# GpSimd for the low halves of probabilities, ScalarE for centring and scaling, TensorE for seven weight splits: one change to a fused attention, Fourier and MLP kernel

## The chip, the cores and the metric

The kernel runs on one core of a Trainium2 chip. Its time is the device time of the program in microseconds; the time before is the median of 3 runs, 1094.59 us (1094.49 to 1094.82). One more execution was taken by the profiler, and all rows below are from it.

A core has five engines, each with a queue of its own that it works off in order: TensorE (PE for its products, PEld for loading the stationary operand), VectorE (DVE), ScalarE (ACT), GpSimd (POOL) and SyncE (SP), which here issues nearly all DMAs. They wait for each other through semaphores.

## What is computed

```python
# attention, 4 batches x 8 heads, 576 tokens, head size 64
scores = scale * q @ k.T
cum = cumsum(maximum(s, 0));  bias = minimum(-(cum[i] - cum[j]), 0)
scores = where(causal, -1e9, scores + bias)
attn = exp(scores - max);  attn = attn / (sum(attn) + 1e-9)
x = attn @ v                       # heads side by side: 4 x 576 x 512
# first block
u = x + real(fft(fft(x, axis=1), axis=2))
un = (u - mean(u)) / sqrt(var(u) + 1e-6)
u2 = u + maximum(un @ w_ch1, 0) @ w_ch2          # 512 -> 2048 -> 512
# second block
xn = (u2 - mean(u2)) / sqrt(var(u2) + 1e-6) * g_ln
out = u2 + maximum(xn @ w2_ch1, 0) @ w2_ch2
```

The weights arrive as 64 bit floats, the rest as 32 bit floats.

## The kernel before

*Two halves for every number.* Most products run in fp16. A number is held as a high half (its fp16 cast) and a low half (what the cast lost, again fp16), and a product is three products: high by high, high by low, low by high. So there are many pairs of instructions of one shape: ScalarE makes the high half, and VectorE or GpSimd subtracts it from the 32 bit value to make the low half.

*Weights.* The class `Weights` handles the first MLP's weights in 32 pieces of 128x512 (16 of `w_ch1`, 16 of `w_ch2`). `prep` loads each piece as 64 bit words into one of nine staging places, turns it into 32 bit floats with three integer instructions on VectorE (L159, L162, L165), squares it on ScalarE for a common power of two as scale (L176), and calls `split` (L203 on ScalarE for the high half with the scale, L204 on VectorE for the low half, scaled and subtracted in one instruction). `prep` is a generator; its steps are put between the steps of the first batch's attention. The second MLP's weights go through the subclass `Weights7`, whose sums of blocks (seven products in place of eight) GpSimd makes (L304).

*Attention.* A batch is four pairs of heads; a pair is 10 units, one for each of five tiles of queries (A0, A1, M, B1, B0, numbered 0 to 4, with 129, 257, 320, 448 and 576 keys) and each of two heads. For a unit, `emit_bias` writes the masked sums into a score tile on GpSimd (L739, for the batches 1 to 3), three units ahead; `emit_qk` multiplies (fp32 in the batches 0 and 1, L1018; split fp16 in 2 and 3, L756 and L757) and VectorE adds the bias and takes the minimum (L1023, L758); `emit_exp` runs the exponential twice on ScalarE, into the fp16 high half (L781) and in place in fp32 with its sum (L782). One unit later `emit_lo` subtracts the two (L794): on GpSimd for the tiles that `KN["LO_POOL"]` names for the batch, on VectorE for the others. A transposing DMA on SP's queue turns the halves (L798, L806), and five or seven units later `emit_pv` multiplies with v (L826) into one PSUM bank, from which VectorE takes the result (L839). In the batches 2 and 3 the sums must carry the scale of q and k: `scale_cum` multiplies the loaded sums in place (L655), and GpSimd's L739 reads them. Where a tile has fewer keys than its blocks, GpSimd clears the rest of the tile (L775) once the tile's last transpose is through.

*Fourier step and LayerNorm.* `fft_steps` does a batch's transform as products with constant matrices. `emit_ln` normalizes a chunk of up to two tiles of 128 tokens: VectorE takes mean and variance (L338, L339) and an estimate of the inverse root (`p`); VectorE makes the centred and scaled 32 bit tile `un` (L351), ScalarE the same in fp16 from the input (L355), VectorE the low half (L358), and a transposing DMA turns both.

*Streams.* `MlpStream` multiplies a chunk with `w_ch1` (L387), applies the relu and splits (L393 on ScalarE, L394 on VectorE), and multiplies with `w_ch2` (L411). Beside the MLP of batch b run the attention and Fourier steps of the next batches, put between the MLP's steps at a fixed rate. After the last batch's MLP has begun, the second MLP's weights are prepared beside it; then nine chunks run through the second MLP (L453, L481).

*Order.* The program's order is only a priority. A planner that weighs every instruction by its own costs, and knows of the priorities and of the `issue_after` and `urgent` blocks, writes down the queue of each engine at build time. An instruction that is moved to another engine so also changes the order of its neighbours.

Of the kernel before, what the change touches and what calls it, by code (L numbers as in the profile page):

```python
# [26 lines left out]
EXT = [129, 257, 320, 448, 576]  # L27
NKB = [2, 3, 3, 4, 5]
MASKED = -(2.0 ** 120)
KN = {'PVS': (0, 3, 0, 0), 'ORD': ((0, 0, 0), (0, 0, 0), (1, 0, 0), (1, 0, 0)), 'WR4': (1.2, 1.2, 1.2, 1.2), 'W0': 4, 'WRATE': 1.0, 'W2PRE': 18, 'NCONST': 40, 'HOLDN': 1, 'S1': 4, 'S2': 1, 'S1B': 0, 'COST': (1.0, 1.0, 1.0, 1.0, 1.0), 'POOL1': (), 'POOLB': (0, 1, 2, 3, 4, 5, 6, 7), 'QF': (3, 3, 3, 3, 3, 3, 3, 3, 3, 3, 3), 'QL': (1, 1, 1, 1), 'WCALLS': 2, 'WN': 65, 'SPGATE': 0, 'LATE4': 1, 'MARK': 30, 'CJ': (2, 6), 'PVLAG': 7, 'LOLAG': 1, 'PVLAG32': 5, 'PJ32': 4, 'A0OFF': 0, 'A1OFF': 0, 'F0OFF': 300, 'AOFF': (200, 0, 300, 300), 'FOFF': (300, 600, 300, 150), 'LNOFF': (300, 600, 150, 600), 'LOFF': 300, 'PJ': 1, 'PN': 1, 'PL': 6, 'KPREP': 0, 'KPRE': (6, 0, 0), 'KSTEP': ((0, 0, 1), (0, 1), (1,)), 'RATES': (1.9, 1.4, 2.1, 1.2), 'POOLX': (0, 1, 1, 1), 'LO_POOL': ((0, 4, 1, 3, 2), (0, 1, 2, 3), (4,), (0, 1, 2)), 'TAILW': 2, 'LNM': 0, 'LAZY': 8, 'CALLS3': 65, 'N32': 2}  # L30


@with_exitstack
def fused_kernel(ctx: ExitStack, tc, q, k, v, s, wa1, wa2, g_ln, wb1, wb2, tok_c, feat_c, ident_c, rev_c, bias_c, out):
    nc = tc.nc
# [75 lines left out]
    class Weights:  # L111
# [3 lines left out]

        PLACE = [i % 9 for i in range(16)] + [6, 5, 4, 3, 7, 8, 6, 5, 7, 8, 6, 7, 8, 7, 8, 7]

        LIMITS, LAST, HOLD = (11, 15), 16, True

        def __init__(self, pool, pre, w1, w2, g, spare, extra, junk):  # L120
            self.staged = {}
# [56 lines left out]
        def scale(self, w):  # L178
            tot = small.tile([128, 1], F32, tag="wtot", name="wtot")
            nc.vector.tensor_reduce(out=tot, in_=self.fro[:, 16 * w:16 * w + 16], op=ALU.add, axis=AX)  # L180
            all_ = total(tot)
            pow2_scale(self.sc[:, 2 * w:2 * w + 1], self.sc[:, 2 * w + 1:2 * w + 2], all_, self.LIMITS[w])
            if w == 0:
                if self.g is None:
                    self.s1 = [self.sc[:, 0:1]] * KB
                else:
                    nc.vector.tensor_scalar(
                        out=self.gs, in0=self.g, scalar1=self.sc[:, 0:1], scalar2=None, op0=ALU.mult
                    )
# [78 lines left out]
    class Weights7(Weights):  # L268

        LIMITS, LAST, HOLD, PLACE = (10, 14), 8, False, [i % 7 for i in range(32)]

        def __init__(self, pool, pre, w1, w2, g, junk):
            self.staged = {}
# [51 lines left out]
    def emit_ln(ch):  # L327

        n = ch.n
        xs = [ch.get(j) for j in range(n)]
        ch.x = xs
        mv = small.tile([128, 2, 2], F32, tag="mv", name="mv")[:, 0:n, :]
        for j in range(n):
            st = small.tile([128, 6], F32, tag="st", name="st")
            nc.vector.bn_stats(out=st, in_=xs[j])  # L338
            nc.vector.bn_aggr(out=mv[:, j, :], in_=st)  # L339
        va4 = small.tile([128, 8], F32, tag="va", name="va")  # L340
        va, p, d, mp = (va4[:, 2 * i:2 * i + n] for i in range(4))
        nc.vector.tensor_scalar(out=va, in0=mv[:, :, 1], scalar1=1e-6, scalar2=None, op0=ALU.add)
        nc.vector.tensor_scalar(
            out=p.bitcast(I32), in0=va.bitcast(I32), scalar1=-0.5, scalar2=float(0x5F3759DF), op0=ALU.mult, op1=ALU.add
        )
        ch.last = nc.vector.scalar_tensor_tensor(out=mp, in0=mv[:, :, 0], scalar=-1.0, in1=p, op0=ALU.mult, op1=ALU.mult)
        yield
        ch.unT = mpool.tile([128, 8, 256], F16, tag="unT", name="unT")
        for j in range(n):
            un = un_tile[0]()[:, 0:512]  # L350
            nc.vector.tensor_scalar(  # L351
                out=un, in0=xs[j], scalar1=mv[:, j, 0:1], scalar2=p[:, j:j + 1], op0=ALU.subtract, op1=ALU.mult
            )
            u16 = mpool.tile([128, 1024], F16, tag="u16", name="u16")
            nc.scalar.activation(  # L355
                out=u16[:, 0:512], in_=xs[j], func=AF.Identity, scale=p[:, j:j + 1], bias=mp[:, j:j + 1]
            )
            ch.last = nc.vector.tensor_tensor(out=u16[:, 512:1024], in0=un, in1=u16[:, 0:512], op=ALU.subtract)  # L358
            ch.tr = nc.sync.dma_start_transpose(out=ch.unT[:, :, j * 128:(j + 1) * 128], in_=u16)
            yield  # L360

        nc.vector.tensor_tensor(out=d, in0=p, in1=p, op=ALU.mult)
# [224 lines left out]
    def prep_cum():  # L587
# [887 lines left out]
```

## Time and profile before

| | |
|---|---|
| median of 3 runs | 1094.59 us |
| profiled execution | 1095.33 us, its span 1093.6 us |
| TensorE (PE) busy | 967.2 us (88%), 8644 products |
| VectorE (DVE) busy | 720.1 us (66%), 1848 instructions |
| ScalarE (ACT) busy | 580.1 us (53%), 1350 instructions |
| GpSimd (POOL) busy | 415.3 us (38%), 717 instructions |
| mean granted clock of TensorE | 0.95 of full speed |

A share of busy time is a mean over stages with different limits, so the span is cut by what runs in it: up to 165 us the first batch's attention and Fourier step and the first MLP's weights; up to 262 us the second batch's attention beside the first MLP; up to 410 and 550 us the third and the fourth batch's; up to 697 us the rest of the first MLP and the second one's weights; up to 785 us the change over to the second MLP; from there on the second MLP alone. Products overlap, so a busy TensorE is not one at its peak.

### The profile page before, as it was taken

The page shows a single profiled execution, that of the slowest core. Times are in us where ns is not written, and L with a number is a line of the kernel's source. Part 1 is how long each engine was busy: PE and PEld are TensorE (multiplying, and loading weights), DVE is VectorE, ACT ScalarE, POOL GpSimd, SP SyncE. Part 2 cuts the span into 40 slices and gives each one's busy share as a digit, 9 for nine tenths or more (in the row PEclk, how much of TensorE's full clock was granted, in tenths as well). Part 3 has the DMA queues.
Part 4 walks back from the last instruction along what each step waited for, and adds up shares of the span by engine and source line. Part 5 has one row for each costly group of instructions (what it writes and reads, how often), then busy time and mean ns, then how long its engine had stood idle before and what let it go on. Part 6 is the DMA issues. An engine that isn't in the chain of part 4 may idle for free.

```text
span 1093.6 us, 23078 instructions
## 1 busy us (share of the span) xinstructions
PE 967.2 (88%) x8644; PEld 740.8 (68%) x8644; DVE 720.1 (66%) x1848; ACT 580.1 (53%) x1350; POOL 415.3 (38%) x717
## 2 busy tenths in 40 slices
PE   4676379999888899688999998898999999999998
PEld 3454246776665666455766665576888888888887
DVE  5978998656896664965757599867644644552342
ACT  5778559774776653576622255744333334333341
POOL 3425444544242231323311000467545443543452
PEclk9768578999999999898999999999999999999999
DMA  6999956986579980598904297020211111110000
GB/s 177 277 199 264 241 132 136 177 147 132 112 139 204 167 157 1 122 196 138 190 20 151 68 291 252 21 58 1 59 20 47 52 27 53 40 40 20 20 21 21
DMA packets 291369, 125.48 MB, mean 115 GB/s; under 512 B 272952, under 2 KB 273208, under 8 KB 291256
## 3 DMA queue, kind: packets, MB, share of 16 engines
q1 hardware_dynamic: 290616, 121.90, 49.9%
q0 software_dynamic: 640, 2.10, 0.6%
q8 instruction: 68, 1.11, 0.4%
q14 instruction: 45, 0.37, 0.1%
HBM read 61.50 MB, written 9.51 MB: 65 GB/s over the span
## 4 chain that ended last, share of the span: by engine, by line
PE 38%; DVE 10%; POOL 3%; DMA 2%; ACT 1%; issue 1%; SPq 1%; ACTq 0%
PE acc L481 13%; PE g1x L453 7%; PE g L453 7%; PE g L387 4%; PE g L411 4%; POOL wbsums L304 2%; DVE wbbig L313 1%; DVE wbbig L165 1%; DMA wbbig<-in_moe_w_ch_dram 1%; DVE wbbig L162 1%; PE pv L826 1%; DVE h L394 1%; DVE wb L162 1%; DVE wb L165 1%; SPq L798 1%
## 5 line engine op out<-in xcount | busy, mean ns | idle before, releaser
L387 PE MATMUL g<-unT,wa 128*128 128x256 f16 (+1 forms) x1920 | 219.4, 265 | 1.4 <-DVE h L394 0.8
L411 PE MATMUL g<-wa,h 128*128 128x512 f16 x864 | 207.4, 382 | 9.2 <-DVE h L394 5.1
L387 PEld LDWEIGHTS <-wa 128*128 128x128 f16 x1920 | 173.9, 99 | 39.7 <-issue 3.0
L481 PE MATMUL acc<-wbbig,wa 128*128 128x256 f16 x1512 | 178.5, 273 | 6.6 <-DVE wa L467 5.3
L453 PEld LDWEIGHTS <-wb 128*128 128x128 f16 x1728 | 169.1, 98 | 20.2
L467 DVE TENSOR_TENSOR wa<-wa,wa 128x896 f16<-128x896 f32 x72 | 79.2, 1100 | 149.2 <-ACT wa L466 149.2
L481 PEld LDWEIGHTS <-wa 128*128 128x128 f16 x1512 | 147.3, 98 | 25.7 <-DVE wa L467 6.7
L411 PEld LDWEIGHTS <-h 128*128 128x128 f16 x864 | 82.9, 99 | 92.5 <-DVE h L394 8.6
L466 ACT CAST wa<-wa 128x896 f16<-128x896 f32 x72 | 67.4, 938 | 117.3 <-POOL wa L464 117.3
L794 POOL TENSOR_TENSOR p<-sc,p 128x129 f16<-128x129 f32 (+4 forms) x104 | 94.7, 917 | 82.6 <-ACT sc L782 74.8
L781 ACT ACTIVATE p<-sc,mn 128x576 f16<-128x576 f32 (+4 forms) x160 | 90.2, 576 | 58.6 <-DVE mn L1023 16.4
L826 PE MATMUL pv<-v,pT 128*128 128x64 f16 x1632 | 72.8, 202 | 43.4 <-DMA pT<-p 24.0
L826 PEld LDWEIGHTS <-pT 128*128 128x128 f16 x1632 | 66.9, 104 | 62.3 <-DMA pT<-p 31.5
L739 POOL TENSOR_SCALAR_AFFINE_SELECT sc<-cumb 128x129 f32<-128x129 f32 (+4 forms) x120 | 67.4, 573 | 109.7 <-DVE p L794 40.6
L453 PE MATMUL g1x<-unT,wb 128*128 128x256 f16 x864 | 101.5, 273 | 0.0
L453 PE MATMUL g<-unT,wb 128*128 128x256 f16 x864 | 100.9, 273 | 0.0
L463 POOL TENSOR_TENSOR wa<-wa 128x128 f32<-128x128 f32 x72 | 46.2, 642 | 121.2 <-ACT wa L460 121.2
L782 ACT ACTIVATE sc<-sc,mn 128x576 f32<-128x576 f32 (+4 forms) x160 | 91.6, 573 | 1.1
L1018 PE MATMUL s<-qkT 128*128 128x288 f32 (+4 forms) x192 | 74.1, 487 | 3.1 <-DVE wasc L106 1.4
L394 DVE SCALAR_TENSOR_TENSOR h<-g,h 128x512 f16<-128x512 f32 (+1 forms) x80 | 50.6, 633 | 38.0 <-ACT h L393 37.6
L393 ACT ACTIVATE h<-g 128x512 f16<-128x512 f32 (+1 forms) x80 | 43.5, 544 | 59.8 <-PE g L387 59.3
L775 POOL MEMSET p<- 128x128 f16 x64 | 13.0, 204 | 112.5 <-DMA pT<-p 80.3
(224 smaller groups left out, 1536.6 us busy)
## 6 DMA issues: line engine op xcount, KB each, us to landing
wbbig<-in_moe_w_ch_dram SPq DMA_DIRECT2D x32, 512.0 KB
wa<-in_moe_w_ch_dram SPq DMA_DIRECT2D x21, 512.0 KB
cumb<-cumd SPq DMA_DIRECT2D x24, 288.0 KB
xset<-in_moe_w_ch_dram SPq DMA_DIRECT2D x11, 512.0 KB
x2d<-o SPq DMA_DIRECT2D x18, 256.0 KB
raw<-in_v_dram SPq DMA_DIRECT2D x32, 128.0 KB
out_dram<-wa SPq DMA_DIRECT2D x16, 256.0 KB
raw<-in_q_dram SPq DMA_DIRECT2D x48, 64.0 KB
```

What stands on the lines that cost most here:

```text
L387: nc.tensor.matmul(out=ps[:, c * i:c * i + c], lhsT=ch.w.w1(lw, kk, m + i), rhs=ch.unT[:, 4 * lx + kk, 0:c], start=(n == 0), stop=(n == 23),)
L411: nc.tensor.matmul(out=ch.ps[j], lhsT=h[:, lh, c:c + 128], rhs=ch.w.w2(lw, m + i), start=(m + i + n == 0), stop=(m + i == MB - 1 and n == 2),)
L453: nc.tensor.matmul(out=ps, lhsT=ch.w.w1(lw, kk, m + 8 * half), rhs=ch.unT[:, 4 * lx + kk, :], start=(n == 0), stop=(n == 11),)
L466: nc.scalar.copy(out=h[:, 0], in_=r[:, 0:7])
L467: nc.vector.tensor_tensor(out=h[:, 1], in0=r[:, 0:7], in1=h[:, 0], op=ALU.subtract)
L481: nc.tensor.matmul(out=acc[key], lhsT=h[:, lh, ia], rhs=b[:, ib, lw], start=(m == 0 and i == 0 and not second), stop=(m == 7 and i == 2 an ...
L739: nc.gpsimd.affine_select(out=u.f[:, 0:n], in_=P.cumb[u.h][:, 0:n], pattern=[[-1, n]], compare_op=ALU.is_ge, fill=MASKED, base=base, chann ...
L781: nc.scalar.activation(out=u.w[:, 0:n], in_=u.f[:, 0:n], func=AF.Exp, bias=mn, scale=-1.0)
L782: nc.scalar.activation(out=u.f[:, 0:n], in_=u.f[:, 0:n], func=AF.Exp, bias=mn, scale=-1.0, accum_out=u.rs[:, h:h + 1])
L794: eng.tensor_tensor(out=u.w[:, w:w + n], in0=u.f[:, 0:n], in1=u.w[:, 0:n], op=ALU.subtract)
L826: nc.tensor.matmul(out=ps[:, c], lhsT=pT[:, lp * nb + kb, :], rhs=P.v[:, kb, lv, c], start=(n == 0), stop=(n == 3 * nb - 1),)
L1018: nc.tensor.matmul(out=ps, lhsT=P.qT[:, QCOLS[t]], rhs=P.kT[h][:, a:z], start=not pe, stop=not masked,)
```

## The change

- *Low halves of probabilities.* `KN["LO_POOL"]` names the tiles of each batch whose low half GpSimd makes. Batch 0: all five, as before. Batch 1: 0 to 3, as before. Batch 2: all five, before only tile 4 (576 keys). Batch 3: all five, before 0, 1 and 2. That moves 32 + 16 instructions L794 from VectorE to GpSimd.
- *Sums' scaling.* `scale_cum` (16 instructions) is a scaled copy on ScalarE instead of a multiplication on VectorE.
- *LayerNorm.* `mp` is now the negative mean alone. ScalarE makes the centred tile `un` (Identity with `mp` as bias) and then its scaled fp16 cast; VectorE makes the low half with scaling and subtraction in one instruction. L351 on VectorE is gone; of 36 tiles each has one more ScalarE pass.
- *Seven weight pieces.* For the pieces 9 to 15 of the first `w_ch1`, the low half is formed in PSUM: the fp32 piece times an identity matrix that carries the scale, plus the fp16 high half times a negative identity in fp16; ScalarE copies the sum out as fp16. The two PSUM banks used (`g2`) are those of the MLP's second product. Two constants are made beside the identity: `eye_neg` after the first loads, `eye_sc` once the scale is known.

```diff
-'LO_POOL': ((0, 4, 1, 3, 2), (0, 1, 2, 3), (4,), (0, 1, 2))
+'LO_POOL': ((0, 1, 2, 3, 4), (0, 1, 2, 3), (0, 1, 2, 3, 4), (0, 1, 2, 3, 4))
...
                 if self.g is None:
                     self.s1 = [self.sc[:, 0:1]] * KB
+                    nc.vector.tensor_scalar(out=eye_sc, in0=ident, scalar1=self.s1[0], scalar2=None, op0=ALU.mult)
...
+            if 9 <= i < 16 and self.by_pe:
+                nc.scalar.activation(out=dst[:, 0:512], in_=self.raw(i), func=AF.Copy, scale=sc)
+                ps = ps_2.tile([128, 512], F32, tag=f"g2{i % 2}", name="low")
+                nc.tensor.matmul(out=ps, lhsT=eye_sc, rhs=self.raw(i), start=True, stop=False)
+                nc.tensor.matmul(out=ps, lhsT=eye_neg, rhs=dst[:, 0:512], start=False, stop=True)
+                nc.scalar.copy(out=dst[:, 512:1024], in_=ps)
+                return
...
-        ch.last = nc.vector.scalar_tensor_tensor(out=mp, in0=mv[:, :, 0], scalar=-1.0, in1=p, op0=ALU.mult, op1=ALU.mult)
+        ch.last = nc.vector.tensor_scalar(out=mp, in0=mv[:, :, 0], scalar1=-1.0, scalar2=None, op0=ALU.mult)
...
-            nc.vector.tensor_scalar(
-                out=un, in0=xs[j], scalar1=mv[:, j, 0:1], scalar2=p[:, j:j + 1], op0=ALU.subtract, op1=ALU.mult
-            )
+            nc.scalar.activation(out=un, in_=xs[j], func=AF.Identity, scale=1.0, bias=mp[:, j:j + 1])
             u16 = mpool.tile([128, 1024], F16, tag="u16", name="u16")
-            nc.scalar.activation(
-                out=u16[:, 0:512], in_=xs[j], func=AF.Identity, scale=p[:, j:j + 1], bias=mp[:, j:j + 1]
-            )
-            ch.last = nc.vector.tensor_tensor(out=u16[:, 512:1024], in0=un, in1=u16[:, 0:512], op=ALU.subtract)
+            nc.scalar.activation(out=u16[:, 0:512], in_=un, func=AF.Copy, scale=p[:, j:j + 1])
+            ch.last = nc.vector.scalar_tensor_tensor(
+                out=u16[:, 512:1024], in0=un, scalar=p[:, j:j + 1], in1=u16[:, 0:512], op0=ALU.mult, op1=ALU.subtract
+            )
...
-        nc.vector.tensor_scalar(out=P.cumb[h], in0=P.cumb[h], scalar1=P.sc[:, 6:7], scalar2=None, op0=ALU.mult)
+        nc.scalar.activation(out=P.cumb[h], in_=P.cumb[h], func=AF.Copy, scale=P.sc[:, 6:7])
...
+        nc.vector.tensor_scalar(out=eye_neg, in0=ident, scalar1=-1.0, scalar2=None, op0=ALU.mult)
```

## Rows read from the trace of the kernel before

**Rows 1.** Busy us (x instructions) by stage: PE, PEld, DVE, ACT, POOL; PEclk, DMA, GB/s
```profile
165.00:262.00 97.00, 94.24 (x889) 67.40 (x889) 70.27 (x222) 78.77 (x200) 45.70 (x81) 0.97 0.79 147
262.00:410.00 148.00, 130.89 (x1243) 91.97 (x1241) 106.42 (x330) 91.62 (x231) 50.23 (x94) 0.99 0.83 155
410.00:550.00 140.00, 121.02 (x1206) 83.79 (x1203) 92.27 (x305) 79.58 (x206) 46.24 (x89) 0.94 0.69 126
...
620.00:697.00 77.00, 68.42 (x543) 45.15 (x541) 71.61 (x152) 42.14 (x101) 9.30 (x7) 0.98 0.66 205
...
785.00:1093.60 308.60, 302.51 (x2770) 270.67 (x2767) 134.38 (x246) 111.69 (x201) 135.38 (x254) 1.00 0.13 34
```

**Rows 2.** The same view, of 110 to 130 us.
```profile
110.00:130.00 20.00, 5.80 (x102) 5.27 (x102) 19.11 (x42) 11.75 (x32) 10.09 (x8) 0.58 1.02 247
```

**Rows 3.** Waits of 100 to 130 us: who, for whom, us, times, longest.
```profile
PE pv L826 <- DVE xset L839: 10.8, 5, 3.1
...
PE pv L826 <- DVE xm L839: 4.6, 1, 4.6
```

**Rows 4.** Groups by line, VectorE, 107.5 to 126.5 us: count, busy us, mean ns.
```profile
L204 DVE SCALAR_TENSOR_TENSOR wa<-wa,wasc,wa 128x512 f16<-128x512 f32 x7 | 6.2, 879 | 0.0
```

**Rows 5.** Timelines of TensorE (start, us), two stretches; the group of 512 columns.
```profile
18.00 1.17 PE L1018 MATMUL s<-qkT 128*128 128x288 f32 x2
...
103.38 0.92 PE L1018 MATMUL s<-qkT 128*128 128x448 f32 x2
...
L411 PE MATMUL g<-wa,h 128*128 128x512 f16 x864 | 207.4, 382 | 9.2 <-DVE h L394 5.1 <-ACT h L393 3.9 <-DVE o L419 0.3
```

**Rows 6.** Groups by line, whole span: casts, LayerNorm.
```profile
L355 ACT ACTIVATE u<-xset,va 128x512 f16<-128x512 f32 x34 | 26.7, 806 | 23.1 <-DMA unT<-u 16.0 <-DVE va L346 6.5 <-DVE va L362 0.4
L358 DVE TENSOR_TENSOR u<-un,u 128x512 f16<-128x512 f32 x36 | 25.5, 709 | 8.2 <-ACT u L355 7.7
...
L203 ACT ACTIVATE wa<-wa,wasc 128x512 f16<-128x512 f32 x30 | 21.0, 710 | 3.9 <-DVE wa L204 2.1 <-DVE wasc L106 1.6
L351 DVE TENSOR_SCALAR un<-xset,mv,va 128x512 f32<-128x512 f32 x34 | 21.0, 624 | 0.3
```

**Rows 7.** The same view: the sums' scaling, and a ScalarE pass as wide.
```profile
L782 ACT ACTIVATE sc<-sc,mn 128x576 f32<-128x576 f32 x32 | 24.6, 768 | 0.5
...
L655 DVE TENSOR_SCALAR cumb<-cumb,scs 128x576 f32<-128x576 f32 x16 | 8.1, 515 | 11.1 <-DMA cumb<-cumd 11.1
```

**Rows 8.** Waits of 262 to 410 us, and (the last row) of 410 to 550.
```profile
POOL sc L739 <- DVE p L794: 24.5, 13, 5.7
POOL sc L739 <- DVE cumb L655: 22.9, 6, 7.3
POOL p L775 <- DMA pT<-p: 21.4, 10, 5.1
...
PE s L756 <- DVE mn L758: 5.4, 7, 1.6
...
PE s L756 <- DVE mn L758: 11.4, 4, 8.8
```

**Rows 9.** Low halves: GpSimd to 262 us, VectorE to 410 and to 550, GpSimd by form.
```profile
L794 POOL TENSOR_TENSOR p<-sc,p 128x257 f16<-128x257 f32 (+3 forms) x30 | 23.0, 771 | 14.7 <-ACT sc L782 9.0 <-issue 5.5
...
L794 DVE TENSOR_TENSOR p<-sc,p 128x129 f16<-128x129 f32 (+3 forms) x32 | 16.9, 537 | 2.9 <-ACT sc L782 2.8
...
L794 DVE TENSOR_TENSOR p<-sc,p 128x576 f16<-128x576 f32 (+1 forms) x16 | 11.4, 718 | 0.0
...
L794 POOL TENSOR_TENSOR p<-sc,p 128x576 f16<-128x576 f32 x16 | 21.8, 1361 | 23.7 <-ACT sc L782 22.8 <-DVE rs L1066 0.9
L794 POOL TENSOR_TENSOR p<-sc,p 128x448 f16<-128x448 f32 x16 | 19.1, 1191 | 14.7 <-ACT sc L782 14.5
```

**Rows 10.** VectorE's L159: timeline at 92 us, and its group of 617 to 697 us.
```profile
92.03 1.25 DVE L159 TENSOR_SCALAR wa<-wa 128x512 int32<-128x512 int32 x1
...
L159 DVE TENSOR_SCALAR wbbig<-wbbig 128x512 int32<-128x512 int32 x16 | 6.5, 421 | 0.8 <-DMA wbbig<-in_moe_w_ch_dram 0.8
```

More of the change, by code (lines that the diff above doesn't have):

```diff
@@ L29 @@
 MASKED = -(2.0 ** 120)
-KN = {'PVS': (0, 3, 0, 0), 'ORD': ((0, 0, 0), (0, 0, 0), (1, 0, 0), (1, 0, 0)), 'WR4': (1.2, 1.2, 1.2, 1.2), 'W0': 4, 'WRATE': 1.0, 'W2PRE': 18, 'NCONST': 40, 'HOLDN': 1, 'S1': 4, 'S2': 1, 'S1B': 0, 'COST': (1.0, 1.0, 1.0, 1.0, 1.0), 'POOL1': (), 'POOLB': (0, 1, 2, 3, 4, 5, 6, 7), 'QF': (3, 3, 3, 3, 3, 3, 3, 3, 3, 3, 3), 'QL': (1, 1, 1, 1), 'WCALLS': 2, 'WN': 65, 'SPGATE': 0, 'LATE4': 1, 'MARK': 30, 'CJ': (2, 6), 'PVLAG': 7, 'LOLAG': 1, 'PVLAG32': 5, 'PJ32': 4, 'A0OFF': 0, 'A1OFF': 0, 'F0OFF': 300, 'AOFF': (200, 0, 300, 300), 'FOFF': (300, 600, 300, 150), 'LNOFF': (300, 600, 150, 600), 'LOFF': 300, 'PJ': 1, 'PN': 1, 'PL': 6, 'KPREP': 0, 'KPRE': (6, 0, 0), 'KSTEP': ((0, 0, 1), (0, 1), (1,)), 'RATES': (1.9, 1.4, 2.1, 1.2), 'POOLX': (0, 1, 1, 1), 'LO_POOL': ((0, 4, 1, 3, 2), (0, 1, 2, 3), (4,), (0, 1, 2)), 'TAILW': 2, 'LNM': 0, 'LAZY': 8, 'CALLS3': 65, 'N32': 2}
+KN = {'PVS': (0, 3, 0, 0), 'ORD': ((0, 0, 0), (0, 0, 0), (1, 0, 0), (1, 0, 0)), 'WR4': (1.2, 1.2, 1.2, 1.2), 'W0': 4, 'WRATE': 1.0, 'W2PRE': 18, 'NCONST': 40, 'HOLDN': 1, 'S1': 4, 'S2': 1, 'S1B': 0, 'COST': (1.0, 1.0, 1.0, 1.0, 1.0), 'POOL1': (), 'POOLB': (0, 1, 2, 3, 4, 5, 6, 7), 'QF': (3, 3, 3, 3, 3, 3, 3, 3, 3, 3, 3), 'QL': (1, 1, 1, 1), 'WCALLS': 2, 'WN': 65, 'SPGATE': 0, 'LATE4': 1, 'MARK': 30, 'CJ': (2, 6), 'PVLAG': 7, 'LOLAG': 1, 'PVLAG32': 5, 'PJ32': 4, 'A0OFF': 0, 'A1OFF': 0, 'F0OFF': 300, 'AOFF': (200, 0, 300, 300), 'FOFF': (300, 600, 300, 150), 'LNOFF': (300, 600, 150, 600), 'LOFF': 300, 'PJ': 1, 'PN': 1, 'PL': 6, 'KPREP': 0, 'KPRE': (6, 0, 0), 'KSTEP': ((0, 0, 1), (0, 1), (1,)), 'RATES': (1.9, 1.4, 2.1, 1.2), 'POOLX': (0, 1, 1, 1), 'LO_POOL': ((0, 1, 2, 3, 4), (0, 1, 2, 3), (0, 1, 2, 3, 4), (0, 1, 2, 3, 4)), 'TAILW': 2, 'LNM': 0, 'LAZY': 8, 'CALLS3': 65, 'N32': 2}
 @with_exitstack
@@ L116, in fused_kernel @@
         PLACE = [i % 9 for i in range(16)] + [6, 5, 4, 3, 7, 8, 6, 5, 7, 8, 6, 7, 8, 7, 8, 7]
-        LIMITS, LAST, HOLD = (11, 15), 16, True
+        LIMITS, LAST, HOLD, by_pe = (11, 15), 16, True, True
         def __init__(self, pool, pre, w1, w2, g, spare, extra, junk):
@@ L268, in fused_kernel @@
     class Weights7(Weights):
-        LIMITS, LAST, HOLD, PLACE = (10, 14), 8, False, [i % 7 for i in range(32)]
+        LIMITS, LAST, HOLD, by_pe, PLACE = (10, 14), 8, False, False, [i % 7 for i in range(32)]
         def __init__(self, pool, pre, w1, w2, g, junk):
@@ L350, in emit_ln @@
             un = un_tile[0]()[:, 0:512]
-            nc.vector.tensor_scalar(
-                out=un, in0=xs[j], scalar1=mv[:, j, 0:1], scalar2=p[:, j:j + 1], op0=ALU.subtract, op1=ALU.mult
-            )
-            u16 = mpool.tile([128, 1024], F16, tag="u16", name="u16")
-            nc.scalar.activation(
-                out=u16[:, 0:512], in_=xs[j], func=AF.Identity, scale=p[:, j:j + 1], bias=mp[:, j:j + 1]
-            )
-            ch.last = nc.vector.tensor_tensor(out=u16[:, 512:1024], in0=un, in1=u16[:, 0:512], op=ALU.subtract)
+            nc.scalar.activation(out=un, in_=xs[j], func=AF.Identity, scale=1.0, bias=mp[:, j:j + 1])
+            u16 = mpool.tile([128, 1024], F16, tag="u16", name="u16")
+            nc.scalar.activation(out=u16[:, 0:512], in_=un, func=AF.Copy, scale=p[:, j:j + 1])
+            ch.last = nc.vector.scalar_tensor_tensor(
+                out=u16[:, 512:1024], in0=un, scalar=p[:, j:j + 1], in1=u16[:, 0:512], op0=ALU.mult, op1=ALU.subtract
+            )
             ch.tr = nc.sync.dma_start_transpose(out=ch.unT[:, :, j * 128:(j + 1) * 128], in_=u16)
@@ L549, in flush @@
             emit_g2x(self.pend[0][0], *(a[1:] for a in self.pend))
-    ident = xpool.tile([128, DM], F32, tag="xm1", name="ident")[:, 0:128]
+    eyes = xpool.tile([128, DM], F32, tag="xm1", name="eyes")
+    ident, eye_sc, eye_neg = eyes[:, 0:128], eyes[:, 128:256], eyes[:, 256:320].bitcast(F16)
     rev = const.tile([128, 16], I32, name="rev")
```

## The prediction

> **What bounds the kernel now.** I read the busy table by stages first. From 785 us to the end TensorE is busy 302.51 of 308.60 us [rows 1]; nothing that the change touches can shorten that stretch. From 165 to 262 us (the second batch's attention beside the first MLP) it is busy 94.24 of 97.00. It is less full in two stages, 262 to 410 and 410 to 550 us (attention of the third and fourth batch): 17.1 and 19.0 us idle [rows 1]. Between 620 and 697 us VectorE is busy 71.61 of 77.00, and TensorE idles 8.6.
>
> Then the end of the first batch's attention: between 110 and 130 us VectorE is busy 19.11 of 20 us and TensorE 5.80, at a mean granted clock of 0.58 [rows 2], so mostly at the lower of its two levels (1.2 GHz). The waits of 100 to 130 us tell why: the product with v waits 10.8 and 4.6 us for VectorE to empty the one PSUM bank (L839) [rows 3]. So VectorE's queue sets the pace there, and in the later attention stages it is one of several links.
>
> **The change, part by part.**
>
> *Seven weight pieces (9 to 15).* In 107.5 to 126.5 us seven L204 instructions hold VectorE 6.2 us [rows 4]; all seven leave it, right in the stretch that it bounds. Added are two 128x128 constants on VectorE (under 0.6 us each by the 0.515 row of L655, 576 wide [rows 7]), and per piece one fp32 product of 512 columns, one fp16 product of 512 columns and one ScalarE copy out of PSUM. No fp32 product of 512 columns is in the trace. A pair of records of 448 columns takes 0.92 us, one of 288 columns in a slow stretch 1.17 [rows 5]; by columns that is 1.05 or 2.08. The fp16 product is 207.4/864 = 0.24 us [rows 5], or twice that. So 1.29 to 2.56 us a piece, 9 to 18 us in all. The cover is TensorE's idle time: 14.2 us in 110 to 130 us. I take the products as hidden but for some 1 us of pv behind them. ScalarE's copy is at most the 0.71 us of a cast [rows 6], about 5 us, in a stretch where it is busy 11.75 of 20 us [rows 2]. Without the cover the whole 9 to 18 would count. Of the 6.2 us that leave VectorE I keep 3.5: batch 0's Fourier step and LayerNorm follow in the same queue, but their tail also waits for ScalarE, GpSimd and late weight loads.
>
> *LayerNorm (36 tiles).* VectorE loses L351, 624 ns each, 22 us over the program. The subtraction becomes a fused one: 709 ns (L358) to 879 (the seven of L204), so 0 to 6 us come back. ScalarE runs two plain passes of about 710 ns for one of 806 [rows 6]: 36 x 0.61 = 22 us more, and the three steps are now in series, so a tile's chain is some 0.6 us longer. From 785 us on ScalarE is busy 111.69 of 308.60 and each chunk's LayerNorm is made a chunk ahead: 0. Between 620 and 697 us three of them leave VectorE, 1.9 us, of which I keep 0.5, since the weights' transfers come next.
>
> *Sums' scaling (16).* VectorE loses 8.1 us of work and 11.1 us of waiting for the sums' DMA; both go to ScalarE, at about the 768 ns of a 576 wide pass [rows 7], 12.3 us. GpSimd waited 22.9 us for this instruction in the third batch alone [rows 8]. Queued behind it on ScalarE are now the exponentials. Bounds: a gain of part of those 22.9, or a loss of up to 11.1 when ScalarE stands waiting. I count it within the next sum.
>
> *Low halves.* Batches 0 and 1 keep theirs. Batch 2 moves 32 (16.9 us of VectorE), batch 3 moves 16 (11.4 us) [rows 9]. On GpSimd the 32 of batch 1, the same four widths, average 771 ns, so 24.7 us; the 448 and 576 wide ones average 1191 and 1361 ns [rows 9], 8 of each 20.4 us. With the sums and LayerNorm VectorE falls from 106.42 to about 82 us of 148, and from 92.27 to about 75 of 140; GpSimd rises from 50.23 to 75 and from 46.24 to 67. GpSimd's 24.5 us of waiting for VectorE's low halves (before it may overwrite the score tile, L739) [rows 8] turn into its own order. TensorE's waits for VectorE's score step are 5.4 us in the third batch and 11.4 in the fourth [rows 8], 16.8 together; the step itself waits for the bias tile that GpSimd writes after the scaled sums and, in part, after the low halves. I take a third, 5.5, less 1 for longer low halves ahead of the transposing DMAs: 4.5. At best both stages come to the 2.8% idle of the second batch's: 130.89/0.972 + 121.02/0.972 = 259.2 for 288, a gain of 28.8. At worst every added microsecond on GpSimd beyond what VectorE needed, 45.1 - 28.3 = 16.8, reaches TensorE.
>
> The Trainium skill (GPSIMD Engine Reference, Engine selection) tells to keep elementwise work of two inputs on VectorE, as GpSimd is about twice as slow. For the same four widths this trace has 771 against 537 ns [rows 9], the same sign and a smaller factor; by the rule's factor VectorE's 28.3 us would become some 57 (an estimate) instead of 45, and the worst case above 28 instead of 16.8.
>
> *Sum.* The profiled execution took 1095.33 us, 1093.6 of it the span. 1095.33 - 3.5 - 0.5 - 4.5 = 1086.8. The median of the runs is 0.74 below the profiled one: 1086.1, so I forecast 1086. Unknown beside this: the planner sorts every engine's queue anew, and a queue order shifted by one instruction is worth some microseconds in gaps as those of [rows 8].
>
> **Rivals.**
>
> 1. *The idle time of the two stages was VectorE's.* For it: the second batch, with its low halves on GpSimd, leaves TensorE 2.8% idle with GpSimd at 45.7 of 97 us [rows 1]. Against: its products are fp32 and longer, and no transposing DMA feeds them. Half of the 28.8 with the 4 of the rest: 1076.
>
> 2. *Contention eats the relief.* At 92.03 us an L159 on VectorE takes 1.25 us beside a low half on GpSimd; the 16 of a stretch in which GpSimd hardly works average 421 ns [rows 10]. If each of the 48 moved ones holds a VectorE instruction for half of its length, 22 of the 28.3 us come back, and what is left is the weights' gain less a longer wait for ScalarE: 1094, no change that can be measured. The Trainium skill (Advanced Engine Details and Errata, Mode Summary) says that GpSimd shares VectorE's second SBUF port and that the two block each other; the two rows of [rows 10] agree, in one direction.
>
> 3. *GpSimd becomes the bound* (slower). Place: the third batch's attention. GpSimd would be busy 75, wait 21.4 us for transposing DMAs ahead of its memsets (L775) and up to 22.9 for the sums [rows 8]: 119 of 148. It decides once its waits for ScalarE's second exponential, with all low halves queued between biases, fill the other 29. Then the 16.8 us of slower low halves fall on TensorE; less the weights' 3.5 and with half of the batch 3 share hidden, some +7: 1102. Against it: batch 1 as above.
>
> 4. *The products stand in TensorE's way, or ScalarE's new waits do* (slower). The fp16 product waits for ScalarE's cast, and pv queues behind it. At 18 us against 14.2 of cover, and with the gain of 3.5 gone, +4; with the 11.1 us of DMA waits on ScalarE half on the path, +9: 1100.
>
> That the change does not do what it says I exclude but for the first two batches, where the sets of low halves are the same before and after.
>
> **How the numbers follow.** Forecast case (1080 to 1092): 0.45. Rival 1: 0.13. Rival 2: 0.15. Rival 3: 0.15. Rival 4: 0.12. About 0.2%, 2.2 us, is what a measurement of this kernel can tell from no change. Faster: 0.45 + 0.13 = 0.58; the same: 0.15; slower: 0.27. The range takes the forecast, rival 2 and the middle of the others: 1073 to 1102; the likeliest case's own is 1080 to 1092.
>
> **What would show it.** Right: in 107 to 127 us no L204 on VectorE, pv's waits for L839 below 15.4 us, and the point from which TensorE stays busy (it is, from 165 us on) 3 to 4 us earlier; in the stages of batches 2 and 3 TensorE's idle time below 36 us by 3 to 6, no wait of GpSimd's L739 for VectorE's low halves; the last stretch as long as before, near 308. Wrong: GpSimd busy or waiting through the third batch's stage with TensorE waiting for p's transposes; VectorE instructions near twice their shortest time beside GpSimd; ScalarE idle ahead of the sums' scaling; or the start of the MLP not earlier at all, which would say that the weights' DMAs and not VectorE set the first stage.

## The result and the profile after

The changed kernel takes 1081.67 us (median of 4 runs, 1075.16 to 1084.82) where the kernel before takes 1094.54 beside it: a ratio of 0.9867, 95% interval 0.9842 to 0.9893, so 1.1 to 1.6% faster; by the medians the change takes off 12.9 us. The forecast was 1086. The profiled execution took 1079.22 us, its span 1077.4. Single executions of one kernel lie up to 6.5 us from their median here, so a difference of one or two microseconds between two traces proves nothing; the timed ratios decide.

All lines that the diff does not add are a few lines further down: the score step L758 is now L766, GpSimd's bias L739 is L747, the sums' scaling L655 is L663 (on ScalarE), the low halves L794 are L802, pv L826 and L839 are L834 and L847.

The busy table of the changed kernel by the stages of [rows 1] and [rows 2], with one stage more (697 to 785 us). After each stretch stand its length, then the busy time of PE, PEld, DVE, ACT and POOL, the granted clock, the DMA share and GB/s:

```profile
110.00:130.00 20.00, 14.52 (x149) 8.38 (x148) 18.74 (x38) 15.69 (x42) 7.96 (x9) 0.78 0.94 222
165.00:262.00 97.00, 95.26 (x903) 68.44 (x903) 68.48 (x214) 79.45 (x201) 46.12 (x81) 0.97 0.79 146
262.00:410.00 148.00, 133.55 (x1255) 93.54 (x1253) 91.49 (x284) 100.44 (x247) 71.80 (x126) 0.97 0.82 155
410.00:550.00 140.00, 127.43 (x1284) 87.99 (x1283) 89.84 (x292) 89.06 (x224) 62.56 (x106) 0.96 0.69 128
620.00:697.00 77.00, 68.48 (x563) 46.53 (x562) 71.71 (x155) 50.13 (x112) 12.15 (x10) 1.00 0.61 189
697.00:785.00 88.00, 84.69 (x709) 69.70 (x708) 53.71 (x89) 42.63 (x71) 61.16 (x90) 0.98 0.13 37
785.00:1077.40 292.40, 287.41 (x2633) 257.36 (x2631) 120.75 (x219) 111.34 (x200) 127.59 (x238) 1.00 0.12 34
```

The stage of 697 to 785 us of the kernel before, which the rows ahead of the prediction leave out:

```profile
697.00:785.00 88.00, 82.11 (x669) 64.72 (x667) 63.15 (x102) 44.92 (x75) 53.74 (x77) 1.00 0.11 28
```

The stretches are the same in both tables, not the work in them, as the changed kernel runs ahead. TensorE's idle time in the two later attention stages fell from 17.11 and 18.98 us [rows 1] to 14.45 and 12.57, 9.1 us together. From 697 to 785 us it fell from 5.89 to 3.31. From 165 to 262 us it fell by 1.0, and in the last stretch TensorE is full as before (5.0 us idle of 292.4, before 6.1 of 308.6). In 620 to 697 us nothing moved.

GpSimd's waits of the changed kernel in the third batch's stage (what waited, for what, us in total, times, the longest), beside [rows 8]:

```profile
POOL p L802 <- ACT sc L790: 34.4, 15, 5.1
POOL sc L747 <- ACT cumb L663: 19.8, 7, 8.9
```

The wait of GpSimd's bias for VectorE's low halves, 24.5 us before, is gone. In its place GpSimd waits 34.4 us for ScalarE's second exponential, and it waits for the scaled sums hardly less (19.8 us against 22.9).

### The profile page after: what moved, and what is told of

Its sections match the earlier page's. It is cut to its first block, busy times and chain, and to the rows that moved or that the text cites. A ratio compares the mean times of both kernels' runs of the same rounds, so it can differ in the third digit from the quotient of the medians.

```text
span 1077.4 us, 23148 instructions
## 1 busy us (share of the span) xinstructions
PE 972.9 (90%) x8665; PEld 742.8 (69%) x8665; DVE 677.3 (63%) x1743; ACT 613.3 (57%) x1409; POOL 450.9 (42%) x765
## 4 chain that ended last, share of the span: by engine, by line
PE 54%; DVE 16%; DMA 10%; issue 6%; ACT 5%; POOL 5%; SPq 3%; DVEq 0%; ACTq 0%; POOLq 0%
PE acc L487 13%; PE g L393 10%; PE g L417 9%; PE g1x L459 7%; PE g L459 7%; DMA pT<-p 4%; DMA qkT<-qk 2%; PE pv L834 2%; PE s L1026 2%; DMA wbbig<-in_moe_w_ch_dram 2%; POOL p L802 1%; DVE wa L159 1%; PE y L1134 1%; DVE wa L162 1%; ACT p L789 1%
## 5 line engine op out<-in xcount | busy, mean ns | idle before, releaser
L802 POOL TENSOR_TENSOR p<-sc,p 128x448 f16<-128x448 f32 (+4 forms) x152 | 134.8, 896 | 113.8 <-ACT sc L790 100.7
L789 ACT ACTIVATE p<-sc,mn 128x129 f16<-128x129 f32 (+4 forms) x160 | 90.3, 575 | 36.3 <-DVE mn L766 17.2
L469 POOL TENSOR_TENSOR wa<-wa 128x128 f32<-128x128 f32 x72 | 49.6, 689 | 115.7 <-ACT wa L466 115.7
L834 PEld LDWEIGHTS <-pT 128*128 128x128 f16 x1632 | 65.2, 102 | 44.5 <-DMA pT<-p 26.0
L834 PE MATMUL pv<-v,pT 128*128 128x64 f16 x1632 | 70.4, 199 | 25.8 <-DMA pT<-p 16.8
L790 ACT ACTIVATE sc<-sc,mn 128x129 f32<-128x129 f32 (+4 forms) x160 | 91.6, 573 | 0.9
L747 POOL TENSOR_SCALAR_AFFINE_SELECT sc<-cumb 128x129 f32<-128x129 f32 (+4 forms) x120 | 63.3, 542 | 50.7 <-ACT cumb L663 25.9
L209 POOL TENSOR_TENSOR wb<-wb,wb 128x512 f16<-128x512 f32 x8 | 10.7, 1356 | 109.6 <-DVE wbbig L165 106.0
```

Of the source, the lines that this page charges most:

```text
L747: nc.gpsimd.affine_select(out=u.f[:, 0:n], in_=P.cumb[u.h][:, 0:n], pattern=[[-1, n]], compare_op=ALU.is_ge, fill=MASKED, base=base, chann ...
L789: nc.scalar.activation(out=u.w[:, 0:n], in_=u.f[:, 0:n], func=AF.Exp, bias=mn, scale=-1.0)
L790: nc.scalar.activation(out=u.f[:, 0:n], in_=u.f[:, 0:n], func=AF.Exp, bias=mn, scale=-1.0, accum_out=u.rs[:, h:h + 1])
L802: eng.tensor_tensor(out=u.w[:, w:w + n], in0=u.f[:, 0:n], in1=u.w[:, 0:n], op=ALU.subtract)
L834: nc.tensor.matmul(out=ps[:, c], lhsT=pT[:, lp * nb + kb, :], rhs=P.v[:, kb, lv, c], start=(n == 0), stop=(n == 3 * nb - 1),)
```

## Experiments

### One part at a time

The theories. A: the low halves pay, since VectorE has less to do. B: the sums' scaling pays. C: no part has a worth of its own, since the planner writes every queue anew, and the parts don't add up. Each kernel is the kernel before with one part of the diff.

**Low halves alone:** `LO_POOL` as in the changed kernel, nothing else.

> The kernel before with the low halves of batches 2 and 3 on GpSimd, nothing else. Theory A (the gain is VectorE's relief by the low halves, in the stages of batches 2 and 3): two thirds of the 12.9 us or more, so 1083 to 1087. Theory B (the gain is the scaled sums' earlier arrival at GpSimd): 1092 to 1097, since GpSimd gets more to do and the sums come as late as before. Theory C (each part only makes the planner sort the queues anew, and the gaps fall otherwise): anything within 8 us of 1094.5, with the four single parts not adding up to the whole.

Measured: 1093.08 us (12 runs), ratio 0.9991 (0.9976 to 1.0006). No gain that can be told: A falls. What the 48 moved instructions did, in the stretch of 262 to 550 us of this kernel and then of the kernel before:

```profile
POOL p L794 <- ACT sc L782: 37.3, 20, 4.6
...
PE s L756 <- DVE mn L758: 9.6, 7, 2.8
```

```profile
POOL sc L739 <- DVE p L794: 40.6, 19, 5.7
...
POOL p L794 <- ACT sc L782: 23.7, 10, 6.3
...
PE s L756 <- DVE mn L758: 16.8, 11, 8.8
```

TensorE waits 7.2 us less for the score step, the longest of these waits falls from 8.8 to 2.8 us, and still the timed runs show no gain that can be told (the two traced executions, 1091.32 and 1095.33 us, lie on either side of their medians). So fewer of these waits do not by themselves make the program shorter. The 28.3 us of low halves that leave VectorE (34.3 to 6.0) lower its busy time by 9.9 only (720.1 to 710.2), because other instructions of its own grow (shown under the hardware, below).

**Weight pieces alone:** the branch `if 9 <= i < 16 and self.by_pe` and its constants, nothing else.

> The kernel before with the seven pieces split by identity products, nothing else. The prediction's term says 3.5 us off, 1091. In the changed kernel's trace TensorE was no further with its work at 212 us than before, which says 1094 to 1095 (theory A and B). Theory C: within 8 us of 1094.5.

Measured: 1096.81 us (12 runs), ratio 1.0028 (1.0012 to 1.0043), so a loss of 2.7 us. The first product of the first MLP starts 2.4 us earlier (166.99 against 169.37), but the products of its first chunk end 6.5 us later (254.6 against 248.1), and on the way TensorE stands still for p's transpose in the second batch's attention, a gap that the kernel before does not have (start, duration, engine and line, and in brackets the idle time before it and its releaser):

```profile
217.39 0.82 PE L836 MATMUL pv<-v,pT 128*128 128x64 f16 x12 [3.08 <-DMA pT<-p]
```

That this gap and the late chunk make the loss is not shown: the changed kernel with the old LayerNorm (below) has both, ends its first chunk at 256.1 us, and is still 7 us faster than the kernel before.

**LayerNorm alone:** `emit_ln` as in the changed kernel, nothing else.

> The kernel before with the LayerNorm's centring on ScalarE, nothing else. Theory A and B: 0.5 to 3 us off from the second MLP's weights on (620 to 785 us), so 1091 to 1094, and nothing ahead of 165 us. Theory C: within 8 us of 1094.5.

Measured: 1088.81 us (7 runs), ratio 0.9950 (0.9929 to 0.9971): 5.3 us. TensorE's waits from 697 to 785 us, where the first MLP hands over to the second, in the kernel before, in this one, and in the changed kernel:

```profile
PE acc L481 <- DVE wa L467: 4.6, 3, 2.9
PE acc L481 <- DVE wa L489: 0.8, 1, 0.8
PE acc L481 <- ACT wa L466: 0.5, 1, 0.5
```

```profile
PE acc L479 <- DVE wa L465: 2.1, 3, 1.0
PE acc L479 <- ACT wa L464: 1.5, 1, 1.5
...
```

```profile
PE acc L487 <- DVE wa L473: 1.7, 2, 1.0
PE acc L487 <- ACT wa L472: 1.5, 1, 1.5
```

The second MLP's second product waits for the low half that VectorE makes (L467 before), and in VectorE's queue the LayerNorm of the next chunk lies ahead of it. The kernel before, with the centring close in front of the low half that ends the longest of these waits (2.87 us):

```profile
743.35 1.03 DVE L351 TENSOR_SCALAR un<-xset,mv,va 128x512 f32<-128x512 f32 x1
...
744.89 1.08 DVE L467 TENSOR_TENSOR wa<-wa,wa 128x896 f16<-128x896 f32 x1
```

With the centring on ScalarE the waits for it fall from 4.6 to about 2 us, while those for ScalarE's cast rise from 0.5 to 1.5. TensorE's idle time in this stretch falls by 1.5 us (5.89 to 4.41), so most of the 5.3 lies elsewhere. The trace's largest fall is in the fourth batch's attention: 18.98 to 11.75 us in 410 to 550 us.

**Sums' scaling alone:**

```diff
-nc.vector.tensor_scalar(out=P.cumb[h], in0=P.cumb[h], scalar1=P.sc[:, 6:7], scalar2=None, op0=ALU.mult)
+nc.scalar.activation(out=P.cumb[h], in_=P.cumb[h], func=AF.Copy, scale=P.sc[:, 6:7])
```

> The kernel before with the sums' scaling on ScalarE, nothing else. Theory A: 1093 to 1097 (waits move from VectorE to ScalarE). Theory B: 1084 to 1088, with the 8.8 us gap of TensorE at 449 us mostly gone. Theory C: within 8 us of 1094.5.

Measured: 1085.38 us (6 runs), ratio 0.9923 (0.9902 to 0.9945): 8.7 us, two thirds of the whole change, from 16 instructions. B has the size right and the reason wrong. GpSimd does not wait less for the scaled sums; in 262 to 550 us it waits longer, 38.9 us in this kernel (first fence) against 30.7 before (second):

```profile
POOL sc L739 <- ACT cumb L655: 38.9, 11, 8.3
...
ACT cumb L655 <- DMA cumb<-cumd: 3.9, 4, 1.9
```

```profile
POOL sc L739 <- DVE cumb L655: 30.7, 8, 7.3
...
DVE cumb L655 <- DMA cumb<-cumd: 11.1, 6, 3.1
```

What is gone is the 11.1 us that VectorE stood waiting for the sums' DMA. B had also expected the long gap of TensorE near 449 us to be mostly gone; it is still 7.96 us. And waits are not all of it. Between these two traces lie 12.0 us; 5.0 of them are idle time of TensorE (126.3 to 121.4 us) and 7.1 busy time (967.2 to 960.1), on the same 8644 products. In 410 to 550 us its granted clock is 0.98 here and 0.94 before.

### Parts in company

The four single effects (-1.0, +2.7, -5.3, -8.7 us) sum to -12.3, close to the whole (-12.9), which speaks against C. The next runs test whether that is more than chance. Three kernels are the changed one less a part, one is the kernel before with two.

> The changed kernel with its weight pieces 9 to 15 split on VectorE again (no products, no two added constants); the other three parts stay. Theory D (the parts add up, and the products cost what they cost alone, +2.7 us): 1079 us, 2 to 3 us under the changed kernel's 1081.7, and the first product of the MLP about 2 us later but the end of the first MLP earlier. Rival E (the products pay once VectorE is relieved by the other parts, as the prediction's 3.5 us had it): 1084 to 1086. Rival F (the products neither cost nor give anything, and the +2.7 was the planner's new order): 1081 to 1082.

Changed kernel without the weight pieces: 1084.73 us (6 runs), ratio 0.9915 (0.9890 to 0.9940). The products that cost 2.7 us alone give some 3 to 5 here: between 0.9915 and 0.9867 lie 4.8 thousandths, where the two intervals together allow 3.6 for chance; the medians differ by 3.1 us.

> The kernel before with two of the four parts: the sums' scaling and the LayerNorm's centring on ScalarE. Theory D (the parts add up): -8.7 and -5.3 give 1080 us, with the last stretch as long as before and the gain made in the fourth batch's attention (about -8 by 500 us) and at the start of the second MLP (a further -4). Rival E (both remove the same waits of VectorE's queue in the fourth batch's attention, so that they overlap): 1084 to 1086, no better than the sums' scaling alone.

Sums' scaling and LayerNorm: 1087.42 us (8 runs), ratio 0.9943 (0.9924 to 0.9963). Adding would have given 1080; the pair is no better than the scaling alone.

> The changed kernel with the sums' scaling back on VectorE. Theory D (the parts add up): 1090 us, and GpSimd's waits for the scaled sums in the third batch's attention back at some 23 us. Rival E (in the changed kernel VectorE is so much relieved by the low halves and the LayerNorm that it can do the scaling in time): 1082 to 1085, with those waits below 15 us.

Changed kernel with the scaling back on VectorE: 1092.24 us (12 runs), ratio 0.9983 (0.9968 to 0.9998). The other three parts together are worth 1.6 us without the scaling, so in this company the scaling is worth 10.6. GpSimd's waits for the sums were not back at 23 us for that (15.3 in both stages).

> The changed kernel with the LayerNorm as before (VectorE's centring, ScalarE's one pass). Theory D (the parts add up): 1087 us, the 5 us lost by the start of the second MLP at about 740 to 800 us of the span. Rival E (the LayerNorm's gain is the fourth batch's late score step, which the sums' scaling removes as well): 1082 to 1083.

Changed kernel with the LayerNorm as before: 1086.85 us (7 runs), ratio 0.9940 (0.9918 to 0.9963), a loss of 5.2 us against the changed kernel by the medians, 8 by the ratios, where the part alone gave 5.3. The 3 us gap of pv that the pieces alone brought is here too (3.13 us, at 220 us) and is absent from the changed kernel: in the five kernels with these products it stands in the two where VectorE still centres, and in none of the three others.

So the parts do not add up; that the sum of the single effects fitted was chance. The scaling helps alone and in the changed kernel, the LayerNorm too but not beside the scaling alone, the products change their sign, and the low halves show nothing by themselves. C is right that far, which leaves the question whether the move of an instruction pays or the new order.

### The move and the order, apart

Moving the 16 scalings changes the order of every queue from the second batch's Fourier step on. These kernels hold the order: at the end of the program every instruction is tied to its forerunner in a list of the other build, by an edge of issue order without a wait. The traces show the order held: but for the 16 scalings TensorE, VectorE and ScalarE work off the same instructions in the same sequence as the build that lent it (in the fourth kernel TensorE, and SyncE's DMAs). No kernel was run held in its own order, so what the edges cost by themselves is not known.

```diff
+    keep_order(tc)
...
+                tc.add_manual_dep(
+                    ins[place], last.name,
+                    mybir.DependencyInfo(mybir.DependencyClass.NoSync, mybir.DependencyReason.DATA), reason="order",
+                )
```

> The kernel before with the sums' scaling on ScalarE, and every queue held in the order that the planner wrote for the kernel before (edges of issue order alone, no waits); only the 16 scalings change their engine, and the planner places them in ScalarE's queue. Theory M (the move itself pays: VectorE loses 8.1 us of work and 11.1 us of waiting, the rest follows): as with the free order, 8 to 9 us under the kernel before, 1085. Theory O (what paid was the new order that the planner wrote for all queues once 16 instructions had another engine): within 2.5 us of the kernel before, 1091.5 to 1096.5, with TensorE's wait of some 8 us at 448 us still there.

The scaling on ScalarE in the old order: 1090.75 us (9 runs), ratio 0.9971 (0.9960 to 0.9982), 3.1 us.

> The work of the kernel before, the scaling on VectorE, but every queue held in the order that the planner wrote for the kernel with the scaling on ScalarE; the 16 scalings are placed by the planner in VectorE's queue. Theory M (the move pays): no gain, 1092 to 1096. Theory O (the order pays): most of the gain without any move, 1085 to 1088. Each a part: between 1088 and 1092.

The scaling on VectorE in the order that was written for it on ScalarE: 1095.16 us (12 runs), ratio 1.0014 (0.9999 to 1.0029), no gain.

> The changed kernel with the sums' scaling back on VectorE, every queue held in the order that the planner wrote for the changed kernel. With a free order this took 1092.2 us. Theory M: that again, 1089 to 1093. Theory O: within 2.5 us of the changed kernel, 1079 to 1084.

The scaling back on VectorE in the changed kernel's order: 1089.47 us (12 runs), ratio 0.9953 (0.9935 to 0.9970), a loss of 7.8 us by the medians (9.4 by the ratios) with nothing else moved.

> The kernel before with three parts of the change (low halves, LayerNorm's centring, sums' scaling; the weight pieces stay on VectorE), TensorE's and SyncE's queues held in the order of the kernel before, the other queues free. With all queues free this took 1084.7 us, 9.1 below the kernel before. Theory M: 1084 to 1087. Theory O (the order of products and transfers pays): 1090 to 1095. If both hold in part: 1087 to 1090.

Three parts in the old order of TensorE and SyncE: 1091.24 us (12 runs), ratio 0.9982 (0.9965 to 0.9998), 2.6 us where the free order gives 9.1.

Neither theory holds by itself. The move alone gives 3.1 us, the order alone nothing, both 8.7; and in the changed kernel's order, which was written for the move, taking it back costs 7.8. The longest gap of the kernel before stays in the old order. The score product of the fourth batch after its gap, in the kernel before, in the old order with the scaling moved, and in the changed kernel:

```profile
457.53 0.40 PE L756 MATMUL s<-qkT,qx 128*128 128x288 f16 x1 [8.77 <-DVE mn L758]
```

```profile
457.04 0.40 PE L756 MATMUL s<-qkT,qx 128*128 128x288 f16 x1 [8.70 <-DVE mn L758]
```

```profile
446.27 0.28 PE L764 MATMUL s<-qkT,qx 128*128 128x288 f16 x1 [2.31 <-DVE mn L766]
```

In the old order TensorE still stands 8.70 us there. But the gap does not tell why the old order keeps most of the loss: the kernel with the scaling alone, in a free order, has it too (7.96 us) and gains elsewhere. Which part of the order matters is open.

The same place in two kernels whose orders agree shows what the move itself does. The changed kernel's order with the scaling on VectorE, its queue and then TensorE's:

```profile
476.28 0.52 DVE L663 TENSOR_SCALAR cumb<-cumb,scs 128x576 f32<-128x576 f32 x1 [2.25 <-DMA cumb<-cumd]
...
479.36 0.52 DVE L663 TENSOR_SCALAR cumb<-cumb,scs 128x576 f32<-128x576 f32 x1 [2.10 <-DMA cumb<-cumd]
...
480.76 0.57 DVE L766 CUSTOM_DVE_ANT_0 sc<-s,sc,mn 128x288 f32<-128x288 f32 x1
```

```profile
481.39 0.27 PE L764 MATMUL s<-qkT 128*128 128x257 f16 x1 [3.21 <-DVE mn L766]
```

The changed kernel itself, VectorE's, ScalarE's and TensorE's queue at that place:

```profile
473.79 0.57 DVE L766 CUSTOM_DVE_ANT_0 sc<-s,sc,mn 128x288 f32<-128x288 f32 x1
```

```profile
476.88 0.78 ACT L663 ACTIVATE cumb<-cumb,scs 128x576 f32<-128x576 f32 x1 [1.80 <-DMA cumb<-cumd]
```

```profile
476.18 0.27 PE L764 MATMUL s<-qkT 128*128 128x257 f16 x1
```

On VectorE the two scalings stand 2.25 and 2.10 us for their DMAs, and the score step L766 is queued behind both; TensorE needs the score bank that this step empties and waits 3.21 us. On ScalarE the scaling stands 1.80 us, but the score step does not wait behind it, and TensorE has no gap. Over 262 to 550 us, the kernel with the scaling on VectorE and then the changed one:

```profile
DVE cumb L663 <- DMA cumb<-cumd: 14.3, 7, 3.5
...
PE s L764 <- DVE mn L766: 11.6, 10, 3.2
...
POOL sc L747 <- DVE cumb L663: 7.0, 4, 3.3
```

```profile
POOL sc L747 <- ACT cumb L663: 25.9, 11, 8.9
...
ACT cumb L663 <- DMA cumb<-cumd: 5.4, 3, 2.0
...
PE s L764 <- DVE mn L766: 4.9, 5, 2.3
```

TensorE's waits for the score step fall by 6.7 us and its idle time in this stretch by 4.8 (31.83 to 27.02), of the 7.8 of the runs, although GpSimd waits 18.9 us more for the sums. None of the twelve kernels is faster than the changed one.

Open: what the low halves are worth in company (the changed kernel without them was not run; 0.9915 with them and 0.9943 without, both without the weight pieces, can't be told apart), which orders make the products pay, and what in an order is worth the difference between 3.1 and 8.7 us.

## Why the prediction was right, and where it was not

The time was inside the likeliest case's own range (1080 to 1092), and the sign was right. The size was 8.5 us forecast against 12.9 measured. The terms were not right, so that the time fell so near is in part luck: two terms were sized too small, and the third came out near its size, but not by the road forecast.

**Weight pieces, -3.5.** Their local steps came out. The waits of pv at the end of the first batch's attention, and the products (busy us, mean ns, and idle time before them), of the changed kernel in 100 to 135 us:

```profile
L834 PE MATMUL pv<-v,pT 128*128 128x64 f16 x190 | 8.6, 205 | 6.5 <-DVE xset L847 3.9 <-DVE xm L847 1.3 <-DMA pT<-p 1.3
L202 PE MATMUL low<-wa,eyes 128*128 128x512 f32 x10 | 7.3, 819 | 0.0
...
L203 PE MATMUL low<-wa,eyes 128*128 128x512 f16 x7 | 3.4, 488 | 0.0
```

pv waits 5.2 us for VectorE where it waited 15.4 [rows 3]; the products of all seven pieces take 12.9 us (14 fp32 records 9.5, four of them ahead of this stretch, and seven fp16 ones 3.4), inside the 9 to 18; the MLP's first product is 2.1 us earlier. The step that failed is the last one, "I keep 3.5": the first chunk's products end at 248.3 us against 248.1, so nothing of that lead reaches the end of the chunk. Nor is the lead the pieces' alone. The MLP starts at 167.0 us with the pieces alone, but at 166.3 to 166.6 in the three kernels with the new LayerNorm and no pieces in a free order, and at 169.7, as before, with the pieces and the old LayerNorm. So the time that VectorE gave back there was not the bound of what follows. In the changed kernel the pieces are worth 3.1 us by the medians, near the 3.5, but they lose 2.7 alone; with the forecast road not there, this match is luck. Where they gain and where they lose is not shown. Rival 4 (the products stand in the way) had the sign right for the pieces alone and not the mechanism: 12.9 us of products are less than the 14.2 of cover, and the new gap stands in the next batch's attention, behind a transposing DMA.

**LayerNorm, -0.5.** Mis-sized: 5.3 alone, 5.2 by the medians (8 by the ratios) with and without it in the changed kernel. The instructions cost what was forecast:

```profile
L362 DVE SCALAR_TENSOR_TENSOR u<-un,va,u 128x512 f16<-128x512 f32 x36 | 31.4, 871 | 22.2 <-ACT u L361 22.2
...
L361 ACT ACTIVATE u<-un,va 128x512 f16<-128x512 f32 x36 | 25.4, 712 | 8.6 <-DMA unT<-u 8.5
...
L359 ACT ACTIVATE un<-xset,va 128x512 f32<-128x512 f32 x34 | 24.0, 717 | 22.3 <-DVE va L354 9.6 <-DVE u L362 7.1 <-DVE va L351 2.8
...
L663 ACT ACTIVATE cumb<-cumb,scs 128x576 f32<-128x576 f32 x16 | 11.9, 764 | 5.5 <-DMA cumb<-cumd 5.4
```

The fused low half is at the upper bound (871 of 709 to 879), the plain passes at 712 and 717, the scaling at 764 (forecast 768). What was missed is a stage: the rows went from 620 to 697 and from 785 on, and the stretch between, where TensorE waits for VectorE's low halves, was not read. There the whole change saves 2.6 us (5.89 to 3.31 idle). From the end of the first MLP's last product to the end of the program, the six traces with the new LayerNorm in an order written for it take 361.65 to 361.75 us, and the seven with the old one 363.64 to 364.47: 2 to 3 us of the part are made there, in every company. (With TensorE's old order held, the new LayerNorm takes 364.11.) The rest lies ahead of it, where the forecast had counted VectorE's relief by the LayerNorm only within the 4.5 us of the next paragraph.

**Sums' scaling and low halves, -4.5.** The place was right (TensorE's idle time in two stages, forecast 3 to 6 us less, measured 9.1 less), and the split was wrong: the scaling gave most (8.7 us alone, 10.6 when it is taken out of the changed kernel), the low halves by themselves nothing. The step that failed is "GpSimd waited 22.9 us for this instruction", the price put on an earlier arrival at GpSimd. The other number of the same paragraph was the one: the 11.1 us that VectorE stood for the DMA with the score step behind it. Of the 16.8 us of TensorE's waits for that step [rows 8] a third was taken; in the changed kernel 11.9 went. That these waits alone set the price is not shown, since the low halves by themselves took off 7.2 of them for no gain.

**The rivals.** Rival 1: half of the 28.8 us was asked for and 9.1 came. Rival 2 (contention eats the relief, no change) is what the low halves did alone: 18.4 of 28.3 us came back to VectorE (forecast 22), and its busy time fell by 9.9. Rival 3: GpSimd is busy 71.80 of 148 us (forecast 75), and its waits for ScalarE's second exponential are 34.4 us, more than the 29 that were to decide. So its condition was met, and its consequence did not follow: TensorE waits 4.9 us for p's transposes in that stage where it waited 7.5. An engine whose stage is full of waits need not be one that others wait for. ScalarE's new waits, the other half of rival 4, were 5.4 us and not 11.1. Two of the recorded sums do not come out: rival 3's terms (16.8 less 3.5, less half of batch 3's 9.0) give +8.8 and not +7, and rival 4's +9 on 1094.6 gives 1104 and not 1100. They bear on the upper end of the range alone.

## What to carry to other kernels

Price an instruction that waits for a DMA by what is queued behind it on its engine, not only by who reads its result: here the cheaper place for it was the queue with the less urgent work behind it. An in-order queue that a planner writes anew has to be measured with the move, and a part's worth in one company says little of the next; holding the old order and moving one instruction, then the reverse, shows how far the two can be told apart. And read every stage between the start and the end before a term is called nought.

## What the runs showed of the hardware

GpSimd's low halves lengthen some of VectorE's instructions and not others. Groups of VectorE in 262 to 550 us (busy us, mean ns), in the kernel before and in the one with the low halves alone, GpSimd having 48 instructions more:

```profile
L394 DVE SCALAR_TENSOR_TENSOR h<-g,h 128x512 f16<-128x512 f32 x30 | 20.5, 684 | 13.8 <-ACT h L393 13.8
...
L692 DVE SCALAR_TENSOR_TENSOR qk<-raw,scs,qk 128x320 f16<-128x320 f32 x16 | 9.0, 564 | 0.0
...
L708 DVE COPY qx<-qkT 128x512 f16<-128x512 f16 x8 | 2.3, 294 | 9.8 <-DMA qkT<-qk 9.8
```

```profile
L394 DVE SCALAR_TENSOR_TENSOR h<-g,h 128x512 f16<-128x512 f32 x30 | 20.4, 681 | 14.0 <-ACT h L393 13.9
L692 DVE SCALAR_TENSOR_TENSOR qk<-raw,scs,qk 128x320 f16<-128x320 f32 x16 | 11.5, 726 | 0.0
...
L708 DVE COPY qx<-qkT 128x512 f16<-128x512 f16 x8 | 4.0, 502 | 14.2 <-DMA qkT<-qk 14.2
```

In the mean L692, which reads two tiles in SBUF, grows by 29% and the copy L708 by 71%; L394, which reads one of its two tiles from PSUM, stays the same, and so does the score step (448 wide: 674 and 677 ns), which reads PSUM too. But the growth is not spread over the group. Of the eight copies five stay at 294 ns and three take 740, 883 and 925; of the sixteen L692 three (882, 1551 and 1562 ns) make up most of the rise. Each of these six runs beside a low half on GpSimd, as the longest of the copies does here:

```profile
360.95 0.93 DVE L708 COPY qx<-qkT 128x512 f16<-128x512 f16 x1 [1.00 <-DMA qkT<-qk]
```

```profile
360.68 1.04 POOL L794 TENSOR_TENSOR p<-sc,p 128x448 f16<-128x448 f32 x1
```

A copy that runs wholly beside GpSimd's bias L739 (at 329.04 us) takes 294 ns. Not every meeting costs: a copy of the changed kernel at 328.00 us takes 294 ns with a low half beside it for its whole length. The prediction's rival let each moved instruction hold up any of VectorE's; the rows show a few long meetings and only with some instructions. The Trainium skill (GPSIMD Engine Reference, Specifications) names instructions of a 2-port mode or with two SBUF inputs as the ones that contend. The rows of L692 agree; whether the copy runs in such a mode no run shows.

The price of a weight piece on TensorE depends on the stretch it falls in. Its fp32 product, two records together, takes 1.10 us at 112.34 us of the changed kernel's trace, where the granted clock is 0.99 (112 to 120 us), and 1.91 and 2.06 us at 126.96 and 124.68, where it is 0.50 (124 to 129 us), the lower of the two levels.

A long gap of TensorE costs more than its own length. In the kernel before, the granted clock after the gap of 8.77 us is 0.50 (457.5 to 460 us), and 1.00 again from 462.5; the first product takes 0.40 us there, and 0.28 after the shorter gap of the changed kernel at the same place.
